# Loads of q, k and v: one DMA over 128 partitions in place of two over 64 each

## The chip, the cores and the metric

One core of a Trainium2 chip runs the kernel. The metric is the device time of the program in microseconds (us). A core has TensorE (PE, with its weight loads shown apart as PEld), VectorE (DVE), ScalarE (ACT), GpSimd (POOL), and SyncE (SP), which here only issues DMAs.

## What is computed

Sigmoid attention over 8 batches of 12 heads, 448 positions and 64 dimensions a head, and then a gated feed-forward block on its result:

```python
def _attn_ref(q, k, v) -> np.ndarray:
    S = q.shape[2]
    scale = 1.0 / np.sqrt(q.shape[-1])
    scores = scale * np.matmul(q, k.transpose(0, 1, 3, 2)) - np.log(S)
    attn = 1.0 / (1.0 + np.exp(-scores))
    return np.matmul(attn, v).astype(np.float32)
...
def _moe_ref(x, w_gate, w_val, w_out) -> np.ndarray:
    g = x @ w_gate
    silu = g * (1.0 / (1.0 + np.exp(-g)))
    val = x @ w_val
    return (silu * val @ w_out).astype(np.float32)
```

x, (3584, 768), is the attention's output with the heads of a position side by side; the weights are 768x1536, 768x1536 and 1536x768.

## The kernel before

**Tiles.** The unit of the attention is a pair set i: four neighbouring heads of one batch (24 sets, three to a batch; QB = 3, NQ = 24). Positions are laid out as 64 partitions times NS = 7: partition p holds positions 7p to 7p + 6 of a head. A tile of q, k or v holds a set as [128, 2, 7, 64] in float32: partition half g and index a tell the head. In the kernel before, head 4r + 2g + a of the batch stands at half g and index a (r is the set's number in its batch); each half is loaded by a DMA of its own (`load`).

**Casts.** q and k are cast to bf16 into a `src` tile (`cast_qk`: DVE and ACT for set 0, DVE for sets 1 and 2, POOL from set 3), v to fp16 (`cast_v`, always POOL; the cast itself is line 199 of `cp`). Weights are cast by POOL as well (lines 250 and 272).

**Attention.** q and k are transposed so that the head's dimensions stand on partitions (64a to 64a + 63 for index a): on PE for sets 0 to 5 (`tr_pe`, line 284), by a DMA transpose issued from SP for the others (`tr_dma`, line 300). For each of the 7 slots s of the keys `burst` makes four score products (line 317) on the four 64x64 quarters of the array: rows by a, columns by g, the result of index a in bank a of the score tile. `sig` (line 331, ACT) takes the sigmoid of both banks at once. `pv` (line 348) multiplies with v, again four products a slot, 28 a set, added up over s in two banks; each of the two banks becomes a tile xT of 128 features (two heads) by 448 positions, cast by DVE or ACT.

**Feed-forward.** `f1` makes, for a batch and one of 12 chunks of 128 hidden features, six products for the gate and six for the value (line 384); ACT, DVE and DVE again (lines 390, 394, 400) make hT of them. `f2` (line 442) multiplies with the output weights, for two batches at a time.

**Order.** The code lists all operations; `list_schedule` orders them by planned durations, slots of the tile rings and a planned DMA time. Each engine then runs its row in order. The DMAs of SP run in this order: q, k and v of sets 0 to 2; then for c = 0 to 3 six loads of weights (384 of the 1536 hidden features) and q, k, v of one more set; from set 6 on a DMA transpose of a set, the loads of the next, and three loads of output weights (sets 7 to 10). Loads land in a ring of 11 staging tiles ("st"), which casts give back; at most 8 DMAs of SP are on their way, a ninth waits for the landing of the first.

Of the kernel before, what the change touches and what calls it, by code (L numbers as in the profile page):

```python
# [9 lines left out]
FP32 = mybir.dt.float32  # L10
FP16 = mybir.dt.float16
# [123 lines left out]
def kernel(  # L135
# [10 lines left out]
    nc = tc.nc  # L146

    B, H, S, D = q.shape
# [4 lines left out]
    NS = 7  # L153
# [8 lines left out]
    psum = ctx.enter_context(tc.tile_pool(name="ps", bufs=1, space=bass.MemoryType.PSUM))  # L162
    one = ctx.enter_context(tc.tile_pool(name="one", bufs=1))
    stg = ctx.enter_context(tc.tile_pool(name="stg", bufs=1))
    sb = ctx.enter_context(tc.tile_pool(name="sb", bufs=1))
    ctx.enter_context(tc.manual_schedule())

    slots = {"A": 2, "TO": 2, "G": 2, "st": 11, "src": 2,
             "v16": 3, "qkT": 3, "pt": 10, "xT": 14, "osb": 2}
# [18 lines left out]
    def op(*a, **kw):  # L188
        o = Op(*a, **kw)
        ops.append(o)  # L190
        return o

    def cp(eng, o, i):
        if eng == "ACT":
            nc.scalar.copy(out=o, in_=i)
        elif eng == "DVE":
            nc.vector.tensor_copy(out=o, in_=i)  # L197
        else:
            nc.gpsimd.tensor_copy(out=o, in_=i)  # L199


    T = {}
    R = {}

    def load(i, nm, src):

        b, r = divmod(i, QB)

        def part(g):
            def fn():  # L210
                if g == 0:
                    T["st_" + nm, i] = stg.tile([128, 2, NS, D], FP32, tag="st", bufs=slots["st"],
                                                name=f"st_{nm}{i}")
                h = 4 * r + 2 * g
                nc.sync.dma_start(  # L215
                    out=T["st_" + nm, i][64 * g:64 * g + 64],
                    in_=src[b][h:h + 2].rearrange("a (p s) d -> p a s d", s=NS))
            return op("SP", 0.5, fn, take=["st"] if g == 0 else [], desc=(128, NS * D * 4))
        R["st_" + nm, i] = [part(0), part(1)]

    def cast_qk(i, nm, eng, parts=None):

# [10 lines left out]
            for e, s0, s1 in parts]  # L233

    def cast_v(i, eng):
        def fn():
            T["v16", i] = sb.tile([128, 2, NS, D], FP16, tag="v16", bufs=slots["v16"], name=f"v16_{i}")
            cp(eng, T["v16", i], T["st_v", i])
        R["v16", i] = op(eng, 0.98, fn, deps=R["st_v", i], take=["v16"], give=R["st_v", i][0].take)

    def load_w(w, dst, c, j2, nm):
        def fl():
# [64 lines left out]
    def burst(ds):  # L307


        def fpe():  # L310
            for i, s in ds:
                sc = psum.tile([128, 2, 512], FP32, tag="A", bufs=2, name="ps_sc")
                qT, kT = T["qkT", i][:, 0], T["qkT", i][:, 1]
                for g in range(2):
                    for a in range(2):
                        r = slice(64 * a, 64 * a + 64)
                        nc.tensor.matmul(  # L317
                            out=sc[64 * g:64 * g + 64, a, 0:S].rearrange("k (s p) -> k s p", s=NS),
                            lhsT=kT[r, s, 64 * g:64 * g + 64], rhs=qT[r, :, 64 * g:64 * g + 64],
                            start=True, stop=True)  # L320
                T["sc", i, s] = sc
        give = [x for i, s in ds if s == NS - 1 for x in R["qkT", i][0].got("qkT")]
        a = op("PE", 0.19 * len(ds), fpe, deps=[x for i in {i for i, _ in ds} for x in R["qkT", i]],
               mode=("Q", "Q"), take=["A"] * len(ds), give=give)
        for n, d in enumerate(ds):
            sig(d, a, a.take[n])

    def sig(key, a, slot):
        def fn():
            pt = sb.tile([128, 2, S], FP16, tag="pt", bufs=slots["pt"], name="pt")  # L330
            nc.scalar.activation(out=pt, in_=T[("sc",) + key][:, :, 0:S], func=SIGM, bias=sb_t,  # L331
                                 scale=qkscale)
            T[("pt",) + key] = pt
        R[("pt",) + key] = op("ACT", 0.95, fn, deps=[a], take=["pt"], give=[slot])

    def pv(i):

        b, r = divmod(i, QB)

        def slots_of(s0, s1):  # L340
            def fn():
                if s0 == 0:
                    for g in range(2):
                        T["pv", i, g] = psum.tile([128, S], FP32, tag="TO", bufs=2, name="ps_pv")
                for s in range(s0, s1):
                    for g in range(2):
                        for a in range(2):
                            nc.tensor.matmul(  # L348
                                out=T["pv", i, g][64 * a:64 * a + 64, :],
                                lhsT=T["v16", i][64 * g:64 * g + 64, a, s, :],  # L350
                                rhs=T["pt", i, s][64 * g:64 * g + 64, a, :],
                                start=(s == 0), stop=(s == NS - 1))
            return fn

        def fx(g):
            def fn():
                t = sb.tile([128, S], FP16, tag="xT", bufs=slots["xT"], name=f"xT_{b}_{2 * r + g}")
                cp(eng[g], t, T["pv", i, g])
                T["xT", b, 2 * r + g] = t
            return fn  # L360
        eng = ("DVE", "ACT" if r == QB - 1 else "DVE")
        pts = [R["pt", i, s] for s in range(NS)]
        cuts = [0, 5, NS] if i < QB else [0, NS]
        vc = R["v16", i]
        for s0, s1 in zip(cuts, cuts[1:]):
            a = op("PE", 0.19 * (s1 - s0), slots_of(s0, s1), deps=pts[s0:s1] + [vc, R.get(("pv", i))],
                   mode=("Q", "Q"), take=["TO", "TO"] if s0 == 0 else [],
                   give=[x for o in pts[s0:s1] for x in o.take] + (vc.take if s1 == NS else []))
            if s0 == 0:
                banks = a.take  # L370
            R["pv", i] = a
        for g in range(2):
            R["xT", b, 2 * r + g] = op(eng[g], 0.62, fx(g), deps=[a], take=["xT"], give=[banks[g]])
# [115 lines left out]
    def loads(i):  # L489
        for nm, src in (("q", q), ("k", k), ("v", v)):  # L490
            load(i, nm, src)

    def casts(i):
        for nm in "qk":
            cast_qk(i, nm, "DVE" if i < CDVE else "POOL")
        cast_v(i, "POOL")
# [5 lines left out]
    cast_qk(0, "k", None, [("DVE", 0, 4), ("ACT", 4, NS)])  # L502
    tr_pe(0, 1)
    cast_v(0, "POOL")

    for what in ORDER:
# [78 lines left out]
    while fpos < B * NF:  # L585
        b, f = divmod(fpos, NF)
# [41 lines left out]
```

## Time and profile before

| | us |
|---|---|
| median of 3 runs (lowest, highest) | 460.97 (460.84, 461.14) |
| the profiled execution | 460.97 |
| its span in the profile | 459.2 |
| PE busy in the span | 427.3 |
| ACT, DVE, POOL busy | 225.1, 168.9, 109.6 |

The span is the stretch from the first to the last instruction of the profiled execution. The table by stage has, after a stage and its length, the busy time of PE, PEld, DVE, ACT and POOL with their instructions. A busy engine counts instructions only, not waits for semaphores. The granted clock is the share of TensorE's full speed (2.4 GHz) that was granted, 0.5 being 1.2 GHz; the record of it begins at about 21 us, and before that the table by stage shows 1.00. The DMA share is the mean busy share of the core's 16 DMA engines; transfers overlap, so it can pass 1. "Idle before" in square brackets is the time for which an engine stood still ahead of an instruction, with what released it.

### The profile page before, as it was taken

How to read it: one execution, taken by the hardware profiler on the slowest of the kernel's cores; microseconds unless marked ns; L12 is line 12 of the kernel's file. 1: busy time of each engine (PE TensorE's matmuls, PEld its weight loads, DVE VectorE, ACT ScalarE, POOL GpSimd, SP SyncE). 2: the span in 40 equal slices, each digit the busy share in tenths (PEclk: the TensorE clock that was granted, in tenths of full speed). 3: DMA queues.
4: the chain of work that ended last, by engine and by line, in shares of the span. 5: the costliest groups of instructions: out<-in, count | busy, mean ns of one | idle time of the engine just before them, and what ended most of it. 6: DMA issues, size and time to landing. Idle time of an engine off the chain costs nothing.

```text
span 459.2 us, 7942 instructions
## 1 busy us (share of the span) xinstructions
PE 427.3 (93%) x3252; PEld 211.7 (46%) x3252; DVE 168.9 (37%) x278; ACT 225.1 (49%) x305; POOL 109.6 (24%) x145
## 2 busy tenths in 40 slices
PE   2873799989999999999999999999999999999995
PEld 1431344444454554554454554554454545554563
DVE  1512354444433333343434333433334333334210
ACT  3782367865646446455546446445546443112111
POOL 1245464443334233020412133111300000000000
PEclk9998799999999999999999999999999999999999
DMA  8999987999989988518859967528701111110144
GB/s 190 260 286 281 267 260 166 276 249 237 264 184 194 156 186 210 128 68 136 126 132 169 127 130 194 131 67 148 121 1 35 36 36 34 36 47 23 34 104 104
DMA packets 65348, 66.97 MB, mean 146 GB/s; under 512 B 36640, under 2 KB 61472, under 8 KB 65312
## 3 DMA queue, kind: packets, MB, share of 16 engines
q1 hardware_dynamic: 63584, 59.39, 58.5%
q0 software_dynamic: 1728, 7.08, 7.0%
q8 instruction: 25, 0.41, 0.4%
q14 instruction: 11, 0.09, 0.1%
HBM read 47.19 MB, written 11.01 MB: 127 GB/s over the span
## 4 chain that ended last, share of the span: by engine, by line
PE 75%; DMA 19%; SPq 3%; POOL 1%; DVE 1%; ACT 1%; issue 0%; POOLq 0%
PE ps_g L384 20%; PE ps_v L384 20%; PE ps_o L442 19%; DMA st_v<-in_v_dram 7%; PE ps_sc L317 6%; PE ps_pv L348 5%; PE ps_ol L442 5%; DMA st_q<-in_q_dram 5%; DMA st_wv<-in_moe_w_val_dram 3%; DMA st_k<-in_k_dram 3%; SPq L215 2%; DMA qkT<-src 1%; DVE t L394 1%; ACT s L390 1%; POOL v L199 0%
## 5 line engine op out<-in xcount | busy, mean ns | idle before, releaser
L331 ACT ACTIVATE pt<-ps_sc,sbiast 128x896 f16<-128x896 f32 x168 | 159.3, 1005 | 38.7 <-PE ps_sc L317 38.6
L384 PE MATMUL ps_v<-xT,wv 128*128 128x448 f16 x576 | 126.8, 356 | 0.1
L384 PE MATMUL ps_g<-xT,wg 128*128 128x448 f16 x576 | 125.0, 353 | 1.2 <-DVE t L394 1.2
L390 ACT ACTIVATE s<-ps_g 128x448 f16<-128x448 f32 x96 | 52.2, 543 | 123.6 <-PE ps_g L384 123.6
L394 DVE TENSOR_TENSOR t<-ps_g,s 128x448 f16<-128x448 f32 x96 | 60.0, 625 | 126.1 <-ACT s L390 126.1
L442 PE MATMUL ps_o<-wo,hT 128*128 128x384 f16 x528 | 92.5, 326 | 0.0
L442 PEld LDWEIGHTS <-hT 128*128 128x128 f16 x672 | 65.8, 98 | 45.7
L400 DVE SCALAR_TENSOR_TENSOR hT<-ps_v,t 128x448 f16<-128x448 f32 x96 | 60.0, 625 | 61.7 <-PE ps_v L384 60.0
L384 PEld LDWEIGHTS <-wg 128*128 128x128 f16 x576 | 54.7, 98 | 56.9 <-issue 9.8
L384 PEld LDWEIGHTS <-wv 128*128 128x128 f16 x576 | 51.3, 98 | 62.4 <-issue 23.0
L317 PE MATMUL ps_sc<-qkT 64*64 64x448 bf16 x672 | 52.3, 375 | 6.0 <-ACT pt L331 3.4
L463 POOL DMA_DIRECT2D out_dram<-osb x36 | 18.7, 525 | 112.6 <-issue 77.7
L199 POOL CAST src<-st_q 128x896 bf16<-128x896 f32 x21 | 19.6, 934 | 85.2 <-DMA st_q<-in_q_dram 84.2
L348 PE MATMUL ps_pv<-pt,v 64*64 64x448 f16 x672 | 38.6, 360 | 0.6 <-ACT pt L331 0.5
L317 PEld LDWEIGHTS <-qkT 64*64 64x64 bf16 x672 | 14.4, 107 | 38.6 <-issue 33.3
L197 DVE CAST xT<-ps_pv 128x448 f16<-128x448 f32 x40 | 23.4, 619 | 22.5 <-PE ps_pv L348 22.5
L199 POOL CAST v<-st_v 128x896 f16<-128x896 f32 x24 | 22.4, 935 | 38.6 <-DMA st_v<-in_v_dram 23.5
L453 ACT ACTIVATE osb<-ps_o 128x384 f32<-128x384 f32 x22 | 10.8, 490 | 39.8 <-PE ps_o L442 39.8
L348 PEld LDWEIGHTS <-v 64*64 64x64 f16 x672 | 19.8, 109 | 16.0 <-issue 4.8
L284 PE MATMUL ps_tr<-idn,src 128*128 128x128 bf16 x84 | 8.6, 258 | 19.2 <-POOL src L199 10.7
L442 PE MATMUL ps_ol<-wo,hT 128*128 128x384 f16 x144 | 24.7, 326 | 0.0
L455 DVE TENSOR_SCALAR osb<-ps_o 128x384 f32<-128x384 f32 x22 | 12.3, 557 | 31.8 <-PE ps_o L442 31.8
(22 smaller groups left out, 80.6 us busy)
## 6 DMA issues: line engine op xcount, KB each, us to landing
st_q<-in_q_dram SPq DMA_DIRECT2D x48, 224.0 KB, 4.9
st_k<-in_k_dram SPq DMA_DIRECT2D x48, 224.0 KB, 5.1
st_v<-in_v_dram SPq DMA_DIRECT2D x48, 224.0 KB, 5.8
out_dram<-osb POOLq DMA_DIRECT2D x36, 192.0 KB, 3.3
st_wg<-in_moe_w_gate_dram SPq DMA_DIRECT2D x12, 384.0 KB, 7.9
st_wv<-in_moe_w_val_dram SPq DMA_DIRECT2D x12, 384.0 KB, 10.0
st_wo<-in_moe_w_out_dram SPq DMA_DIRECT2D x12, 384.0 KB, 6.7
out_dram<-osb SPq DMA_DIRECT2D x18, 192.0 KB, 2.7
```

The source lines that it names most:

```text
L197: nc.vector.tensor_copy(out=o, in_=i)
L199: nc.gpsimd.tensor_copy(out=o, in_=i)
L317: nc.tensor.matmul(out=sc[64 * g:64 * g + 64, a, 0:S].rearrange("k (s p) -> k s p", s=NS), lhsT=kT[r, s, 64 * g:64 * g + 64], rhs=qT[r, :, ...
L331: nc.scalar.activation(out=pt, in_=T[("sc",) + key][:, :, 0:S], func=SIGM, bias=sb_t, scale=qkscale)
L348: nc.tensor.matmul(out=T["pv", i, g][64 * a:64 * a + 64, :], lhsT=T["v16", i][64 * g:64 * g + 64, a, s, :], rhs=T["pt", i, s][64 * g:64 * ...
L384: nc.tensor.matmul(out=T[nm, b, f], lhsT=w[c][:, j, ff * 128:(ff + 1) * 128], rhs=T["xT", b, j], start=(j == 0), stop=(j == KC - 1))
L390: nc.scalar.activation(out=t, in_=T["g", b, f], func=SIGM)
L394: nc.vector.tensor_tensor(out=t, in0=T["g", b, f], in1=T["s16", b, f], op=MULT)
L400: nc.vector.scalar_tensor_tensor(out=T["hT", m, f][:, o * S:(o + 1) * S], in0=T["v", b, f], scalar=HSC, in1=T["t1", b, f], op0=MULT, op1=MULT)
L442: nc.tensor.matmul(out=o, lhsT=T["hT", m, f][:, t * 128:(t + 1) * 128], rhs=wo16[f][:, cs], start=(f == 0), stop=(f == NF - 1))
L455: nc.vector.tensor_scalar_mul(T["osb", m, t][:, c], o, HREC)
L463: dma.dma_start(out=out[rows, c].rearrange("(p s) d -> s p d", s=NS)[s], in_=T["osb", m, t][64 * n:64 * n + 64, c])
```

## The change

`load` issues one DMA for q, k or v of a set instead of two. The tile's partitions now hold neighbouring heads: head 4r + 2a + g stands at half g and index a, so that each index a is one contiguous piece of 128 x 1792 bytes in DRAM. The planner is told of one DMA of 256 runs instead of two of 128.

Scores: the product of index a and key half g now writes the column half g XOR a (it was g), in bank a as before. So for a = 1 the two halves of the keys' partitions hold the heads in exchanged places.

v: the two halves of index a = 1 are exchanged in the cast to match. `cast_v` does it in three POOL instructions (both halves of a = 0, then each half of a = 1 into the other half), planned at 1.75 instead of 0.98.

Value products: the bank is now given by a and the column half by g, the row half by g XOR a; it was bank and row half by g, column half by a.

```diff
@@ -206,17 +206,12 @@
 
         b, r = divmod(i, QB)
 
-        def part(g):
-            def fn():
-                if g == 0:
-                    T["st_" + nm, i] = stg.tile([128, 2, NS, D], FP32, tag="st", bufs=slots["st"],
-                                                name=f"st_{nm}{i}")
-                h = 4 * r + 2 * g
-                nc.sync.dma_start(
-                    out=T["st_" + nm, i][64 * g:64 * g + 64],
-                    in_=src[b][h:h + 2].rearrange("a (p s) d -> p a s d", s=NS))
-            return op("SP", 0.5, fn, take=["st"] if g == 0 else [], desc=(128, NS * D * 4))
-        R["st_" + nm, i] = [part(0), part(1)]
+        def fn():
+            T["st_" + nm, i] = stg.tile([128, 2, NS, D], FP32, tag="st", bufs=slots["st"], name=f"st_{nm}{i}")
+            nc.sync.dma_start(
+                out=T["st_" + nm, i].rearrange("q a s d -> q a (s d)"),
+                in_=src[b][4 * r:4 * r + 4].rearrange("(a g) (p s) d -> (g p) a (s d)", a=2, s=NS))
+        R["st_" + nm, i] = [op("SP", 0.5, fn, take=["st"], desc=(256, NS * D * 4))]
 
     def cast_qk(i, nm, eng, parts=None):
 
@@ -233,10 +228,13 @@
             for e, s0, s1 in parts]
 
     def cast_v(i, eng):
+
         def fn():
-            T["v16", i] = sb.tile([128, 2, NS, D], FP16, tag="v16", bufs=slots["v16"], name=f"v16_{i}")
-            cp(eng, T["v16", i], T["st_v", i])
-        R["v16", i] = op(eng, 0.98, fn, deps=R["st_v", i], take=["v16"], give=R["st_v", i][0].take)
+            t = T["v16", i] = sb.tile([128, 2, NS, D], FP16, tag="v16", bufs=slots["v16"], name=f"v16_{i}")
+            cp(eng, t[:, 0], T["st_v", i][:, 0])
+            for g in range(2):
+                cp(eng, t[64 - 64 * g:128 - 64 * g, 1], T["st_v", i][64 * g:64 * g + 64, 1])
+        R["v16", i] = op(eng, 1.75, fn, deps=R["st_v", i], take=["v16"], give=R["st_v", i][0].take)
 
     def load_w(w, dst, c, j2, nm):
         def fl():
@@ -315,7 +313,7 @@
                     for a in range(2):
                         r = slice(64 * a, 64 * a + 64)
                         nc.tensor.matmul(
-                            out=sc[64 * g:64 * g + 64, a, 0:S].rearrange("k (s p) -> k s p", s=NS),
+                            out=sc[64 * (g ^ a):64 * (g ^ a) + 64, a, 0:S].rearrange("k (s p) -> k s p", s=NS),
                             lhsT=kT[r, s, 64 * g:64 * g + 64], rhs=qT[r, :, 64 * g:64 * g + 64],
                             start=True, stop=True)
                 T["sc", i, s] = sc
@@ -340,16 +338,15 @@
         def slots_of(s0, s1):
             def fn():
                 if s0 == 0:
-                    for g in range(2):
-                        T["pv", i, g] = psum.tile([128, S], FP32, tag="TO", bufs=2, name="ps_pv")
+                    for a in range(2):
+                        T["pv", i, a] = psum.tile([128, S], FP32, tag="TO", bufs=2, name="ps_pv")
                 for s in range(s0, s1):
                     for g in range(2):
                         for a in range(2):
+                            r = slice(64 * (g ^ a), 64 * (g ^ a) + 64)
                             nc.tensor.matmul(
-                                out=T["pv", i, g][64 * a:64 * a + 64, :],
-                                lhsT=T["v16", i][64 * g:64 * g + 64, a, s, :],
-                                rhs=T["pt", i, s][64 * g:64 * g + 64, a, :],
-                                start=(s == 0), stop=(s == NS - 1))
+                                out=T["pv", i, a][64 * g:64 * g + 64, :], lhsT=T["v16", i][r, a, s, :],
+                                rhs=T["pt", i, s][r, a, :], start=(s == 0), stop=(s == NS - 1))
             return fn
 
         def fx(g):
```

The planned order on PE, ACT and DVE is the same before and after, instruction by instruction. On two engines rows differ.

SP at the start of the program: q, k and v of set 0, q and k of set 1 (names: st_ and the tensor with the number of its set), before

```order
L215 DMA st_q0_99<-in_q_dram 64x2x448 x2
L215 DMA st_k0_103<-in_k_dram 64x2x448 x2
L215 DMA st_v0_106<-in_v_dram 64x2x448 x2
L215 DMA st_q1_109<-in_q_dram 64x2x448 x2
L215 DMA st_k1_114<-in_k_dram 64x2x448 x2
```

SP at the same place, after

```order
L211 DMA st_q0_99<-in_q_dram 128x2x448
L211 DMA st_k0_102<-in_k_dram 128x2x448
L211 DMA st_v0_104<-in_v_dram 128x2x448
L211 DMA st_q1_106<-in_q_dram 128x2x448
L211 DMA st_k1_108<-in_k_dram 128x2x448
```

Nothing moved; each load is one instruction where there were two, and the rest of SP's row follows in the same order.

POOL from q of set 3 to q of set 4 (src: the cast q and k; v16: the cast v; wg and wv: gate and value weights of c = 1), before

```order
L199 CAST src1_73<-st_q3_236 128x2x7x64
L199 CAST src1_73<-st_k3_263 128x2x7x64
L199 CAST v16_3_447<-st_v3_283 128x896
L250 CAST wg16_1_80<-st_wg1_0_303 128x768
L250 CAST wg16_1_80<-st_wg1_1_316 128x768
L250 CAST wg16_1_80<-st_wg1_2_333 128x768
L250 CAST wv16_1_84<-st_wv1_0_344 128x768
L250 CAST wv16_1_84<-st_wv1_1_347 128x768
L250 CAST wv16_1_84<-st_wv1_2_359 128x768
L199 CAST src0_72<-st_q4_391 128x2x7x64
```

POOL on the same stretch, after

```order
L199 CAST src1_73<-st_q3_195 128x2x7x64
L199 CAST src1_73<-st_k3_225 128x2x7x64
L199 CAST v16_3_438<-st_v3_235 128x448
L199 CAST v16_3_438<-st_v3_235 64x448 x2
L248 CAST wg16_1_80<-st_wg1_0_266 128x768
L248 CAST wg16_1_80<-st_wg1_1_307 128x768
L248 CAST wg16_1_80<-st_wg1_2_319 128x768
L248 CAST wv16_1_84<-st_wv1_0_338 128x768
L248 CAST wv16_1_84<-st_wv1_1_348 128x768
L248 CAST wv16_1_84<-st_wv1_2_353 128x768
L199 CAST src0_72<-st_q4_385 128x2x7x64
```

The order is the same; the cast of v has become three instructions, and all that follows stands behind them.

## Rows read from the trace of the kernel before

**Rows 1.** The page, part 4: shares of the chain that ended last, by engine.
```profile
PE 75%; DMA 19%; SPq 3%; POOL 1%; DVE 1%; ACT 1%; issue 0%; POOLq 0%
```

**Rows 2.** Table by stage: length, busy us by engine, granted clock, DMA share, GB/s.
```profile
0.00:33.50 33.50, 20.83 (x218) 10.63 (x218) 9.24 (x16) 22.05 (x25) 8.94 (x17) 1.00 1.00 243
...
33.50:48.40 14.90, 3.72 (x33) 1.92 (x34) 3.12 (x5) 3.41 (x5) 8.13 (x10) 0.78 1.07 276
...
103.00:400.00 297.00, 296.78 (x2252) 145.28 (x2250) 115.63 (x190) 153.58 (x211) 65.16 (x88) 1.00 0.63 127
```

**Rows 3.** Time line of PE: start, length, line, operation, idle before, releaser.
```profile
33.09 0.38 PE L348 MATMUL ps_pv<-pt,v 64*64 64x448 f16 x4 [0.51 <-ACT pt L331]
...
35.94 0.56 PE L284 MATMUL ps_tr<-idn,src 128*128 128x128 bf16 x7 [1.21 <-POOL src L199]
...
38.17 1.30 PE L384 MATMUL ps_g<-xT,wg 128*128 128x448 f16 x6 [0.38 <-DVE t L394]
...
48.38 0.93 PE L284 MATMUL ps_tr<-idn,src 128*128 128x128 bf16 x7 [8.91 <-POOL src L199]
...
49.10 2.45 PE L384 MATMUL ps_v<-xT,wv 128*128 128x448 f16 x6
...
52.19 1.31 PE L384 MATMUL ps_g<-xT,wg 128*128 128x448 f16 x6
```

**Rows 4.** Time line of POOL: casts of v (sets 0, 1) and of q, set 4.
```profile
9.51 0.93 POOL L199 CAST v<-st_v 128x896 f16<-128x896 f32 x1 [8.17 <-DMA st_v<-in_v_dram]
...
15.45 0.93 POOL L199 CAST v<-st_v 128x896 f16<-128x896 f32 x1 [5.02 <-DMA st_v<-in_v_dram]
...
47.39 0.93 POOL L199 CAST src<-st_q 128x896 bf16<-128x896 f32 x1 [1.02 <-DMA st_q<-in_q_dram]
```

**Rows 5.** DMA traffic from 4.5 to 17.5 us, by size of packet.
```profile
DMA packets 1897, 3.03 MB, mean 233 GB/s; under 512 B 208, under 2 KB 1897, under 8 KB 1897
```

**Rows 6.** DMA traffic from 21 to 25.5 us, by size of packet.
```profile
DMA packets 1159, 1.68 MB, mean 373 GB/s; under 512 B 77, under 2 KB 1158, under 8 KB 1158
```

**Rows 7.** Groups of POOL's instructions by shape: count, busy us, mean ns, idle before.
```profile
L199 POOL CAST v<-st_v 128x896 f16<-128x896 f32 x24 | 22.4, 935 | 38.6 <-DMA st_v<-in_v_dram 23.5 <-PE ps_pv L348 10.3 <-issue 3.8
...
L250 POOL CAST wg<-st_wg 128x768 f16<-128x768 f32 x12 | 9.9, 827 | 3.9 <-DMA st_wg<-in_moe_w_gate_dram 3.6
```

**Rows 8.** Time line of ACT: the sigmoids of the first three pair sets.
```profile
10.18 2.80 ACT L331 ACTIVATE pt<-ps_sc,sbiast 128x896 f16<-128x896 f32 x3 [2.27 <-PE ps_sc L317]
...
15.61 2.80 ACT L331 ACTIVATE pt<-ps_sc,sbiast 128x896 f16<-128x896 f32 x3 [0.94 <-PE ps_sc L317]
...
19.54 11.14 ACT L331 ACTIVATE pt<-ps_sc,sbiast 128x896 f16<-128x896 f32 x12 [1.13 <-PE ps_sc L317]
...
31.14 1.90 ACT L331 ACTIVATE pt<-ps_sc,sbiast 128x896 f16<-128x896 f32 x2 [0.46 <-PE ps_sc L317]
```

**Rows 9.** Time line of PE: transposes of k, set 1, and the scores behind them.
```profile
14.11 0.93 PE L284 MATMUL ps_tr<-idn,src 128*128 128x128 bf16 x7 [0.49 <-DVE src L197]
...
14.96 0.96 PE L317 MATMUL ps_sc<-qkT 64*64 64x448 bf16 x8
```

**Rows 10.** Time line of PE: the waits between 57 and 103 us.
```profile
63.37 0.56 PE L284 MATMUL ps_tr<-idn,src 128*128 128x128 bf16 x7 [0.56 <-POOL src L199]
...
80.89 0.38 PE L317 MATMUL ps_sc<-qkT 64*64 64x448 bf16 x4 [0.45 <-DMA qkT<-src]
...
93.73 0.57 PE L317 MATMUL ps_sc<-qkT 64*64 64x448 bf16 x8 [1.26 <-DMA qkT<-src]
```

**Rows 11.** Time line of SP's queue: one DMA transpose.
```profile
86.65 2.83 SPq L300 DMA_TRANSPOSE qkT<-src  x1
```

**Rows 12.** Chain that ended last, in order of time: start us, us, what.
```profile
98.86 5.40 DMA qkT<-src
...
109.93 1.45 PE ps_pv L348 x28
...
122.39 1.45 PE ps_pv L348 x28
```

## The prediction

> **What bounds the kernel now.** I read the chain that ended last first, then the table by stage, then the time lines of TensorE (PE), GpSimd (POOL) and ScalarE (ACT) for the first 110 us, and last the DMA traffic of two short stretches. The profiled execution took 460.97 us, which is also the median of the runs; its span is 459.2, so 1.8 us lie around it, and I add them back at the end.
>
> PE's own work is 75% of the chain that ended last, and 19% of it is DMA [rows 1]. The table by stage tells where [rows 2]. From 103 to 400 us PE stands still for 0.2 us in 297, so nothing is to be had there. The idle time is ahead of that: 12.7 us up to 33.5 and 11.2 between 33.5 and 48.4. There the DMA share is 1.00 and more, and POOL, which casts what has landed, is busy for 8.9 of 33.5 and 8.1 of 14.9 us, so what is late is loads. The largest single gap stands in PE's time line [rows 3]: a product of f1 begins at 38.17 and lasts 1.30, then PE waits 8.91 us for POOL's cast of q of pair set 4 (a pair set is one i, four heads) and begins to transpose it at 48.38. POOL began that cast at 47.39, as soon as the load had landed [rows 4]. In the gap the granted clock falls to 1.2 GHz (0.78 is the mean of that stage, [rows 2]): six f1 products take 2.45 us at 49.10, and 1.31 at 52.19, at 2.4 GHz again [rows 3].
>
> **Why the loads are slow.** Between 4.5 and 17.5 us the queue holds nothing but halves of q, k and v: 3.03 MB in 1897 packets, of which 208 are tiny, so 1792 bytes each, at 233 GB/s [rows 5]. Between 21 and 25.5 it holds weights, 128 partitions a load, 1536 bytes a packet, at 373 GB/s [rows 6]. The DMA engines are full in both. The rows differ in two things, the run length and whether a load goes to 64 or 128 partitions; shorter runs were the faster ones, so I put the difference down to the partitions. POOL's casts of v agree: the first two start 5.94 us apart, which is three loads [rows 4], so 2.0 us for a load of 458,752 bytes, or 229 GB/s.
>
> **The change, part by part.**
>
> *One load over 128 partitions.* Same bytes, same 1792-byte runs, half the number of DMAs. Bounds for the rate are 233 GB/s (nothing gained) and 373; I take 360, near the weights' rate, since the new load has their form. A load then takes 1.27 us. Landing of the n-th load was 3.5 + 2.0n us (v of set 0 is the third, at 9.51), so now 3.5 + 1.27n. For q of set 4, 13 loads and 12 weight loads of 393,216 bytes must have moved, 10.68 MB: 29.7 us at 360, so it lands at 33.2, and with its cast of 0.93 [rows 7] it is ready at 34.1. At 300 GB/s it would be ready at 40.0.
>
> The Trainium skill, SBUF — State Buffer, section "Can I just issue two DMAs to hit both halves?", says that two loads to the two halves serialize, and its section on the DMA port swizzle ("Door 1") gives 196 GB/s for 64 partitions and 328 for 128, at 1 MiB. The trace agrees in direction (233 against 373). By the page's 328 the q would be ready at 37.0, and my total below would grow by 1.5 us.
>
> *What PE does until then.* Whether PE can use it at 34.1 depends on the start. There ACT's sigmoids are the pace, 21 of them, some 0.93 us each (2.80 for three, 11.14 for twelve, [rows 8]). The first, at 10.18, follows from k of set 0, the second load, which now lands at 6.0 instead of 7.5: 8.7, and its bank is free at 9.65. Behind it stand in PE's order a score product, the transposes of q of set 1, a score product, the transposes of k of set 1 and the score product of the fifth sigmoid. The transposes waited for their loads (0.49 us for k, [rows 9]); those now land at 8.6 and 9.9, so nothing there waits for data. At the half rate of these instructions (7 transposes take 0.93 us, as at 48.38) a step with transposes is 0.85 (14.11 to 14.96) and one of a score product 0.65 (14.96 to 15.61): 9.65 + 3 x 0.65 + 2 x 0.85 = 13.3 for the fifth sigmoid, which stood at 15.61, 2.3 us gained. The sigmoids behind it follow at ACT's own pace, and the 0.46 us at 31.14, in which PE stood behind weights being cast, goes too. So the last value products of set 2, at 33.09 [rows 3], come at 30.3 and end at 30.7. From there PE needed 6.0 us to the end of the product of 38.17, of which 1.21 was a wait for k of set 3; I keep 4.8, and PE is at the transposes of set 4 at 35.5. That is later than 34.1, so it decides: **gain 48.38 - 35.5 = 12.9 us.** With full clock earlier in the start it would be up to 14.3 (then the q decides); at 300 GB/s it is 8.4.
>
> *The clock.* Without a gap of 8.91 us I see no cause for the fall to 1.2 GHz (at 31 to 39 us, with waits of up to 1.21 us, the products ran at 2.4). From 48.38 to 52.19 PE did 7 transposes, 6 products and 8 score products; the products took 1.1 us more than at 2.4 GHz, and in the same proportion the rest 0.6: **gain 1.7 us.**
>
> *Later waits.* PE waited 0.56 for q of set 5 and 0.45 and 1.26 for DMA transposes [rows 10]. The latter end a chain on SP: transposes, loads, casts, next transposes; its transposes at 86.65 [rows 11] and 98.86 are 12.2 us apart, as long as PE's own period, from one set's value products to the next, 109.93 to 122.39 [rows 12]. With two loads 0.7 us faster each it is some 1.4 us shorter, and it starts earlier: k of set 6 lands after 18.6 MB, at 55.2, casts end at 57, and transposes take 5.4 us [rows 12], so they are there at 62.5; PE wanted them at 80.4 and, moved by 15.2, does so at 65. **Gain 2.3 us**, bounds 0 and 2.3.
>
> *Cast of v in three pieces.* 128x896 takes 935 ns and 128x768 827 [rows 7], so 0.84 ns a column and 0.18 fixed. A piece of 448 columns is then 0.56 us and three are 1.68; no row shows a cast on 64 partitions or one that moves them, so the bounds are 1.68 and, with 0.93 for each moved piece, 2.43. Nor would it be below 0.93, since no column is left out. POOL's work between v of set 2 (the ninth load, landing now at 14.9) and the cast of q of set 4 is two v, twelve weight casts and two others: 15.2 us (16.7 by the upper bound), so it is through at 30.1 (31.6), before q lands at 33.2. Price 0. If that cover went, it would be 0.75 us a set. Behind a longer cast on POOL stand weight casts and output stores; none of them was late after 103 us.
>
> *SP.* Its order stays, with one issue where two stood , and the next load behind each comes earlier. Price 0: the DMA engines are full.
>
> *Score and value products.* Count, shapes and PE's order stay; what changes is which 64x64 quarter of the array a product uses. 28 value products take 1.45 us [rows 12]; 7 rounds of 448 columns at 2.4 GHz are 1.31, so four quarters run at once. In both kernels the four products of a slot use four different quarters. I take 0, with bounds -0.1 and, if only two could run together, +1.3 us a set.
>
> Sum: 12.9 + 1.7 + 2.3 = 16.9; span 459.2 - 16.9 = 442.3; with 1.8 around it 444.1. **I predict 444 us.**
>
> **The rivals.**
>
> *The value products run two at a time (slower).* Before, the upper half of the array's rows wrote one PSUM bank and the lower half the other. Now each bank (one per a) gets products from both row halves in the same slot, in different column halves. No row shows that case. Rows show the other sharing, two column halves in one bank, at no cost. If the two row halves had to take turns, 24 sets would pay 1.3 us each, 31 us in all: 460.97 - 16.9 + 31 = 475. It decides from 0.7 us a set (16.9 / 24). Against it: the four outputs still lie on disjoint halves of partitions per bank. Chance 0.07.
> The Trainium skill, TensorEngine Tiling (Array Packing), section Restrictions and Gotchas, says that different row tiles cannot use the same PSUM bank at once; PSUM — Partial Sum Buffer, section "PSUM bank collisions raise a hardware error", holds that each bank of each partition is a RAM of its own. By the first the time is this rival's, by the second nothing changes.
>
> *The loads don't get faster.* If the 1792-byte runs or the source, not the 64 partitions, set 233 GB/s, q of set 4 lands where it did. One DMA for two frees SP, but the engines were full. POOL's longer cast stays hidden behind the late loads. 461, within 1. Against it: the rate changes with the kind of load in stretches next to each other [rows 5, 6]. Chance 0.04.
>
> *The gap shrinks but another takes its place.* Loads at under 290 GB/s, or a stall in the first 30 us that I did not see: 451 to 459. Chance 0.05.
>
> **How the numbers follow.** My forecast, 440.5 to 451, has 0.84. Its low end is the full clock earlier (-1.4) and value products 0.1 us quicker (-2.4); its high end is 300 GB/s (+4.5) with the later waits kept (+2.3). That range leaves 0.16 out, so it is also the range that I give. About 0.2% is what a measurement of this kernel can tell from no change. Faster by more: 0.84 + 0.05 = 0.89, less 0.01 for a rival that ends at 460 or so: 0.88. Same 0.04. Slower 0.08, the first rival and a share of the second.
>
> **What would show it.** In the changed kernel: 340 to 370 GB/s in the first 17 us and casts of v 3.8 us apart; PE at the transposes of set 4 near 35.5 with no wait over 1.5 us ahead of them; the granted clock at 2.4 GHz through 30 to 60 us; 28 value products in 1.3 to 1.5 us; POOL's pieces near 0.56 us; PE's idle time ahead of the steady part cut by about 14 us. Wrong would be: loads still 2 us apart, value products near 2.6 us, or a new wait of several us between 20 and 60.

## The result, and the profile after

The changed kernel takes 443.18 us, median of four runs (442.80 to 443.43), against 460.90 (460.06 to 461.14) for the kernel before beside it: a ratio of 0.9618, 95% interval 0.9601 to 0.9635. The forecast was 444, with a range of 440.5 to 451. The profiled execution took 443.35 us with a span of 441.6, so 1.75 us lie around the span, as before.

The page of the kernel after: the engines' totals, the granted clock in 40 slices, and the shares of the chain that ended last (the line that answers to [rows 1]). The last line is the clock's row of the kernel before.

```profile
PE 424.7 (96%) x3252; PEld 211.4 (48%) x3252; DVE 168.5 (38%) x278; ACT 224.9 (51%) x305; POOL 127.8 (29%) x193
...
PEclk9999999999999999999999999999999999999999
...
PE 92%; ACT 3%; DMA 2%; DVE 1%; issue 1%; SPq 0%; ACTq 0%
...
PEclk9998799999999999999999999999999999999999
```

PE's share of the chain went from 75% to 92% and that of DMA from 19% to 2%. No slice of the span reads below full clock any more. (For about the first 20 us this row doesn't tell all: it reads full clock there in both kernels, while seven transposes still take 0.93 us at 19.09 and, at 2.4 GHz, 0.56 at 20.27.)

The table by stage of the kernel after, columns as in [rows 2].

```profile
0.00:33.50 33.50, 22.48 (x236) 12.11 (x236) 10.93 (x19) 22.91 (x27) 19.71 (x33) 1.00 0.98 345
33.50:48.40 14.90, 14.53 (x136) 7.09 (x136) 8.02 (x15) 11.05 (x15) 12.58 (x17) 1.00 1.07 375
...
103.00:400.00 297.00, 296.69 (x2212) 146.93 (x2211) 114.66 (x189) 145.58 (x202) 62.22 (x99) 1.00 0.43 105
```

The second column of numbers is PE's busy time: it stands still for 11.0 us in the first stage and 0.4 in the second, where it was 12.7 and 11.2. The DMA engines are as full as before (0.98 and 1.07), and move 345 and 375 GB/s where they moved 243 and 276. Over the first 103 us PE's idle time fell from 26.2 to 11.4 us.

The time line of PE after, around the place where the long gap of [rows 3] stood (start, length, line, operation, and in brackets the idle time before it and what ended that).

```profile
30.80 0.38 PE L347 MATMUL ps_pv<-pt,v 64*64 64x448 f16 x4 [0.51 <-ACT pt L329]
...
34.45 1.29 PE L381 MATMUL ps_g<-xT,wg 128*128 128x448 f16 x6 [0.24 <-DVE t L391]
35.58 0.55 PE L282 MATMUL ps_tr<-idn,src 128*128 128x128 bf16 x7
35.97 1.30 PE L381 MATMUL ps_v<-xT,wv 128*128 128x448 f16 x6
...
37.71 1.31 PE L381 MATMUL ps_g<-xT,wg 128*128 128x448 f16 x6
...
48.16 0.55 PE L282 MATMUL ps_tr<-idn,src 128*128 128x128 bf16 x7
```

The transposes of q of set 4 start at 35.58 instead of 48.38, with no wait ahead of them, and take 0.55 us instead of 0.93, at 2.4 GHz; the products behind them take 1.30 instead of 2.45. The transposes of set 5 (48.16) don't wait either.

GpSimd's time line after, the answer to [rows 4]: the casts of v of sets 0, 1 and 2, each now three pieces, and of q of set 4.

```profile
8.87 2.19 POOL L199 CAST v<-st_v 128x448 f16<-128x448 f32 x3 [7.53 <-DMA st_v<-in_v_dram]
...
12.54 2.25 POOL L199 CAST v<-st_v 128x448 f16<-128x448 f32 x3 [1.48 <-DMA st_v<-in_v_dram]
...
16.16 1.78 POOL L199 CAST v<-st_v 128x448 f16<-128x448 f32 x3 [1.37 <-DMA st_v<-in_v_dram]
...
33.57 0.93 POOL L199 CAST src<-st_q 128x896 bf16<-128x896 f32 x1 [0.48 <-PE ps_v L381]
```

The casts of v are 3.67 and 3.62 us apart, where the first two stood 5.94 apart: 1.22 us for a load instead of 2.0. The q of set 4 is cast by 34.50 instead of 48.32. GpSimd still stands idle for 0.48 us ahead of that cast. The row puts this down to a product of PE, but the load, issued at 24.79, took 8.6 us to land, so it came in at 33.4, and the load is most likely what the cast waited for.

DMA traffic after, from 4.5 to 14 us, in which the queue holds q, k and v alone (it was 4.5 to 17.5 in [rows 5]):

```profile
DMA packets 2021, 3.38 MB, mean 356 GB/s; under 512 B 122, under 2 KB 2021, under 8 KB 2021
```

The time line of ACT after, the answer to [rows 8], the sigmoids of the first three sets:

```profile
8.20 2.80 ACT L329 ACTIVATE pt<-ps_sc,sbiast 128x896 f16<-128x896 f32 x3 [2.26 <-PE ps_sc L315]
...
13.57 2.80 ACT L329 ACTIVATE pt<-ps_sc,sbiast 128x896 f16<-128x896 f32 x3 [0.37 <-PE ps_sc L315]
...
17.51 11.17 ACT L329 ACTIVATE pt<-ps_sc,sbiast 128x896 f16<-128x896 f32 x12 [1.13 <-PE ps_sc L315]
...
28.84 1.90 ACT L329 ACTIVATE pt<-ps_sc,sbiast 128x896 f16<-128x896 f32 x2 [0.17 <-PE ps_sc L315]
```

PE's waits (what it waited for, total, times, longest): the first three of the list after, and two lines of the list before. Neither GpSimd's casts of q and k (10.7 us in three waits before) nor the DMA transposes (1.9 us in three) stand in the list after.

```profile
PE ps_tr L282 <- DVE src L197: 5.8, 3, 4.6
PE ps_sc L315 <- ACT pt L329: 3.2, 6, 0.7
PE ps_g L381 <- DVE t L391: 1.0, 6, 0.2
...
PE ps_tr L284 <- POOL src L199: 10.7, 3, 8.9
...
PE ps_sc L317 <- DMA qkT<-src: 1.9, 3, 1.3
```

The chain that ended last, after: value products, the answer to [rows 12], and the last output products.

```profile
92.32 1.45 PE ps_pv L347 x28
104.78 1.45 PE ps_pv L347 x28
...
433.00 3.91 PE ps_ol L439 x24
```

The value products stood at 109.93 and 122.39, so 17.61 us are gained by here, and the spans differ by 17.6: everything was gained in the first 92 us. From there the two kernels run alike, 12.46 us from one of these two sets to the next in both.

### The profile page after: what moved, and what is told of

Read it like the earlier page. It is cut to its first block, busy times and chain, and to the rows that moved or that the text cites. A ratio compares the mean times of both kernels' runs of the same rounds, so it can differ in the third digit from the quotient of the medians.

```text
span 441.6 us, 7888 instructions
## 1 busy us (share of the span) xinstructions
PE 424.7 (96%) x3252; PEld 211.4 (48%) x3252; DVE 168.5 (38%) x278; ACT 224.9 (51%) x305; POOL 127.8 (29%) x193
## 4 chain that ended last, share of the span: by engine, by line
PE 92%; ACT 3%; DMA 2%; DVE 1%; issue 1%; SPq 0%; ACTq 0%
PE ps_g L381 25%; PE ps_v L381 25%; PE ps_o L439 19%; PE ps_sc L315 9%; PE ps_pv L347 7%; PE ps_ol L439 5%; ACT pt L329 2%; DMA st_q<-in_q_dram 2%; PE ps_tr L282 1%; DVE t L391 1%; ACT s L387 1%; SPq L211 0%; DVE src L197 0%; ACT xT L195 0%; DVE osb L452 0%
## 5 line engine op out<-in xcount | busy, mean ns | idle before, releaser
L381 PE MATMUL ps_v<-xT,wv 128*128 128x448 f16 x576 | 125.5, 354 | 0.0
L199 POOL CAST v<-st_v 64x448 f16<-64x448 f32 (+1 forms) x72 | 41.0, 569 | 32.6 <-PE ps_pv L347 17.6
L315 PEld LDWEIGHTS <-qkT 64*64 64x64 bf16 x672 | 14.2, 107 | 36.0 <-issue 33.4
L450 ACT ACTIVATE osb<-ps_o 128x384 f32<-128x384 f32 x22 | 10.8, 490 | 39.8 <-PE ps_o L439 39.8
L439 PE MATMUL ps_ol<-wo,hT 128*128 128x384 f16 x144 | 24.7, 326 | 0.0
L199 POOL CAST src<-st_k 128x896 bf16<-128x896 f32 x21 | 19.6, 932 | 5.0 <-DMA st_k<-in_k_dram 4.3
```

The source lines that it names most:

```text
L315: nc.tensor.matmul(out=sc[64 * (g ^ a):64 * (g ^ a) + 64, a, 0:S].rearrange("k (s p) -> k s p", s=NS), lhsT=kT[r, s, 64 * g:64 * g + 64], ...
L381: nc.tensor.matmul(out=T[nm, b, f], lhsT=w[c][:, j, ff * 128:(ff + 1) * 128], rhs=T["xT", b, j], start=(j == 0), stop=(j == KC - 1))
L439: nc.tensor.matmul(out=o, lhsT=T["hT", m, f][:, t * 128:(t + 1) * 128], rhs=wo16[f][:, cs], start=(f == 0), stop=(f == NF - 1))
```

## The experiments

Each is the changed kernel with one edit (the last one with two). Four of them (halves, two by index, weights in halves, whole cast) ran beside the kernel before on one chip, where that took 460.60 us in the median of 19 runs (457.19 to 464.25). The other four shared another chip, where it took 459.82 (458.87 to 460.76).

**Every load as two halves of 64 partitions again, all else of the change kept.**

```diff
-        def fn():
-            T["st_" + nm, i] = stg.tile([128, 2, NS, D], FP32, tag="st", ...)
-            nc.sync.dma_start(
-                out=T["st_" + nm, i].rearrange("q a s d -> q a (s d)"),
-                in_=src[b][4 * r:4 * r + 4].rearrange("(a g) (p s) d -> (g p) a (s d)", a=2, s=NS))
+        def part(g):
+            ...
+                nc.sync.dma_start(
+                    out=T["st_" + nm, i][64 * g:64 * g + 64].rearrange("q a s d -> q a (s d)"),
+                    in_=src[b][4 * r:4 * r + 4].rearrange("(a g) (p s) d -> g p a (s d)", a=2, s=NS)[g])
...
+        R["st_" + nm, i] = [part(0), part(1)]
```

> The changed kernel with each load split again into two DMAs over 64 partitions each; the new layout of heads, the cast of v in three pieces and the new quarters of the products stay. Theory (the 64 partitions of a load set its rate): q, k and v move at about 233 GB/s again, casts of v start about 6 us apart in the first 20 us, PE waits 8 to 10 us for q of set 4 near 40 us, total 459 to 462 us. Rival (the gain came from the layout, the products or the order): the total stays at 443 to 446.

Measured: 459.59 us (456.43 to 460.58), ratio 0.9974 (0.9943 to 1.0005): the gain is gone, and what is left of a difference isn't clear of the noise. Its DMA traffic from 4.5 to 17.5 us, the wait of PE in its time line, and its stage from 33.5 to 48.4 us:

```profile
DMA packets 1992, 3.17 MB, mean 244 GB/s; under 512 B 222, under 2 KB 1992, under 8 KB 1992
```

```profile
45.82 0.93 PE L286 MATMUL ps_tr<-idn,src 128*128 128x128 bf16 x7 [8.02 <-POOL src L199]
```

```profile
33.50:48.40 14.90, 5.94 (x41) 2.94 (x39) 3.65 (x6) 2.88 (x4) 9.07 (x12) 0.72 1.08 288
```

The rate, the gap of 8 us and the fall of the clock (0.72 in this stage, transposes at 0.93 us) all return with the halves. The layout of the heads, the cast in three pieces and the order of the value products are those of the changed kernel here. By themselves they are worth at most the 0.6% that the interval leaves, against the 3.8% of the change, so the gain is that of the loads.

**Two loads again, but split by index a, each over all 128 partitions.** Number and size of the DMAs are those of the kernel before, and the runs are the same 1792 bytes.

```diff
+        def part(a):
+            ...
+                nc.sync.dma_start(
+                    out=T["st_" + nm, i][:, a].rearrange("q s d -> q (s d)"),
+                    in_=src[b][h:h + 2].rearrange("g (p s) d -> (g p) (s d)", s=NS))
...
+        R["st_" + nm, i] = [part(0), part(1)]
```

> The changed kernel with each load split by the index a into two DMAs, each over all 128 partitions: as many DMAs of the same size (224 KB) as before the change, with the same limit of 8 on their way, but 128 partitions. Theory (partitions): 350 to 375 GB/s, total 443 to 445 us. Rival (half as many DMAs, or more bytes on their way under the limit of 8, made the loads faster): 233 to 300 GB/s, total 450 to 461.

Measured: 444.16 us (442.66 to 444.31), ratio 0.9645 (0.9586 to 0.9704). Its traffic from 4.5 to 14 us:

```profile
DMA packets 2182, 3.47 MB, mean 365 GB/s; under 512 B 243, under 2 KB 2182, under 8 KB 2182
```

That two loads became one is not what helped, nor that each is twice as large. That a load goes to 128 partitions and not to one half of them is. Whether the count matters or which 64 they are, no run here tells.

**The weights' loads split into halves of 64 partitions; q, k and v as in the changed kernel.**

```diff
-            nc.sync.dma_start(
-                out=T[nm, c, j2],
-                in_=w[j2 * 256:(j2 + 1) * 256, c * CW:(c + 1) * CW].rearrange(
-                    "(j p) f -> p j f", p=128))
+            for n in range(2):
+                nc.sync.dma_start(
+                    out=T[nm, c, j2][64 * n:64 * n + 64],
+                    in_=w[j2 * 256:(j2 + 1) * 256, c * CW:(c + 1) * CW].rearrange(
+                        "(j n p) f -> n p j f", n=2, p=64)[n])
```

> The changed kernel with each load of gate or value weights split into two DMAs over 64 partitions (runs of 1536 bytes as before, 192 KB a DMA); q, k and v as in the change. Theory (partitions, whatever the data and the run length): the weights fall from about 375 to about 233 GB/s, a load of weights takes 1.7 us instead of 1.05, q of set 4 is ready near 40.7 us, PE waits 4 to 6 us there and a little more at sets 5 and 6, total 448 to 452 us. Rival (runs of 1792 bytes, or the layout of q, k and v in DRAM, were the slow part): weights stay above 350 GB/s, total 443 to 444.

Measured: 457.37 us (454.61 to 460.18), ratio 0.9931 (0.9888 to 0.9973). The direction is right, the size is not: nearly the whole gain is lost. Its traffic from 21 to 25.5 us (the weights), PE's two waits, and GpSimd's casts of q, k and v of set 3:

```profile
DMA packets 735, 1.06 MB, mean 235 GB/s; under 512 B 70, under 2 KB 735, under 8 KB 735
```

```profile
45.22 0.93 PE L283 MATMUL ps_tr<-idn,src 128*128 128x128 bf16 x7 [9.69 <-POOL src L199]
...
61.27 0.67 PE L283 MATMUL ps_tr<-idn,src 128*128 128x128 bf16 x7 [2.00 <-POOL src L199]
```

```profile
28.75 0.93 POOL L199 CAST src<-st_q 128x896 bf16<-128x896 f32 x1 [0.18 <-DMA st_q<-in_q_dram]
31.01 0.93 POOL L199 CAST src<-st_k 128x896 bf16<-128x896 f32 x1 [1.33 <-DMA st_k<-in_k_dram]
33.15 1.78 POOL L199 CAST v<-st_v 128x448 f16<-128x448 f32 x3 [1.20 <-DMA st_v<-in_v_dram]
```

The halves make the weights slow, at 235 GB/s, as expected. What was not expected is in the last fence: the q, k and v between them go to 128 partitions, and still land 2.1 to 2.3 us apart, where in the changed kernel the casts of q, k and v of set 4 start 1.2 us apart (33.57, 34.78, 35.96). The half loads in this queue slow the landings of the full loads among them too. So the whole mixture goes at the slow rate (262 GB/s in the first 33.5 us, 247 in the next stage), and pricing each load by its own kind, as I did here, makes such a mixture too cheap.

**The weights' loads split by rows of the weight instead, two loads of 192 KB over 128 partitions**, the control for the run before.

```diff
+            for n in range(2):
+                nc.sync.dma_start(
+                    out=T[nm, c, j2][:, n],
+                    in_=w[j2 * 256 + n * 128:j2 * 256 + (n + 1) * 128, c * CW:(c + 1) * CW])
```

> The changed kernel with each load of gate or value weights split into two DMAs of 192 KB, each over all 128 partitions (by the two row blocks of the load): the count and size of the split into halves of e3, without the 64 partitions. Theory (64 partitions make loads slow): 350 to 375 GB/s up to 33 us, total 443 to 445 us, so that nearly all of the 14 us that e3 lost is due to the partitions. Rival (more DMAs of 192 KB under the limit of 8 on their way leave the DMA engines short of work): total 448 to 457 us, DMA share dips as in e3.

Measured: 443.79 us (442.35 to 444.50), ratio 0.9646 (0.9620 to 0.9673). Its first two stages, columns as in [rows 2]:

```profile
0.00:33.50 33.50, 22.82 (x246) 12.34 (x247) 12.09 (x21) 23.65 (x28) 19.33 (x33) 1.00 0.97 332
33.50:48.40 14.90, 14.85 (x134) 7.27 (x133) 8.14 (x14) 10.73 (x14) 10.95 (x15) 1.00 1.00 337
```

As many weight loads of the same size as in the run before, and the gain is whole: its loss there is due to the 64 partitions. The time is the expected one; the rate, 332 GB/s in the first stage, is below the 350 to 375 that I expected.

**The cast of v in one instruction.**

```diff
-            cp(eng, t[:, 0], T["st_v", i][:, 0])
-            for g in range(2):
-                cp(eng, t[64 - 64 * g:128 - 64 * g, 1], T["st_v", i][64 * g:64 * g + 64, 1])
+            cp(eng, t, T["st_v", i])
```

> The changed kernel with v cast in one instruction of 128x896, without the exchange of halves; it leaves the exchange out, so the value products pair the wrong heads. Theory (POOL's longer cast is covered): total within 0.5 us of the changed kernel, 442.7 to 443.7 us, with POOL busy 18 us less. Rival (the pieces delay weights or transposes): 1 to 3 us faster than the changed kernel.

Measured: 442.90 us (442.57 to 443.27), ratio 0.9625 (0.9568 to 0.9682), beside 0.9618 for the changed kernel. First its page's totals, then the groups of GpSimd's pieces in the changed kernel (busy us, mean ns):

```profile
PE 422.6 (96%) x3252; PEld 210.3 (48%) x3252; DVE 168.6 (38%) x278; ACT 224.7 (51%) x305; POOL 109.9 (25%) x145
```

```profile
L199 POOL CAST v<-st_v 64x448 f16<-64x448 f32 x48 | 27.6, 574 | 2.9
L199 POOL CAST v<-st_v 128x448 f16<-128x448 f32 x24 | 13.4, 560 | 29.7 <-PE ps_pv L347 17.6 <-DMA st_v<-in_v_dram 12.1
```

The three pieces cost GpSimd 41.0 us for 24 sets where the whole cast costs 22.4 (24 times 0.935), and 17.9 us less work on that engine moved the end by nothing that can be measured. The exchange in the cast has no price that shows, as long as GpSimd has the room.

**PSUM banks of the value products given out by row half**, as in the kernel before: each bank is then written from one half of the array's rows only.

```diff
-                                out=T["pv", i, a][64 * g:64 * g + 64, :], lhsT=T["v16", i][r, a, s, :],
+                                out=T["pv", i, g ^ a][64 * g:64 * g + 64, :], lhsT=T["v16", i][r, a, s, :],
```

> The changed kernel with the bank of a value product given by the row half again (g XOR a), so that no bank gets products from both row halves; it leaves the order of the heads wrong in two of four quarters, so the feed-forward part gets its features in another order. Theory (sharing a bank between row halves costs nothing): 28 value products take 1.45 to 1.52 us as in the changed kernel, total within 0.5 us of 443.2. Rival (the sharing has a price): value products quicker and the total 1 us or more below the changed kernel.

Measured: 442.44 us (442.12 to 443.28), ratio 0.9624 (0.9602 to 0.9645). The median is 0.74 us below the changed kernel's, where I expected 0.5 at most, but on another chip; the ratio to the kernel before beside it is the same (0.9618). Value products and the last output products in its chain, and two rows of PE's time line:

```profile
103.58 1.45 PE ps_pv L347 x28
122.71 1.32 PE ps_pv L347 x28
...
431.79 3.91 PE ps_ol L439 x24
```

```profile
14.56 1.14 PE L347 MATMUL ps_pv<-pt,v 64*64 64x448 f16 x20
...
34.36 0.56 PE L282 MATMUL ps_tr<-idn,src 128*128 128x128 bf16 x7 [0.40 <-POOL src L199]
```

Value products take as long as in the changed kernel (1.45 at 104.78, 1.32 at 123.92). From the transposes of set 4 to the last output products, a stretch with the value products of 21 sets, it is 397.43 us here and 397.42 in the changed kernel (35.58 to 433.00). What sets the two profiles 1.2 us apart lies ahead of it: here TensorE ran at 2.4 GHz from about 14 us on, so that the twenty value products of 14.56 take 1.14 us, and 2.13 in the changed kernel (14.96). The banks aren't the reason, since in the run with the whole cast, which has the changed kernel's banks, they take 1.14 too (14.72). So the two row halves writing one bank, in different halves of its partitions, cost nothing that shows, where the rival priced it at 31 us.

**Warm up: 32 products of the identity with itself, before the first data.**

```diff
+    ps_w = psum.tile([128, 512], FP32, tag="G", bufs=2, name="ps_w")
+    for n in range(32):
+        nc.tensor.matmul(out=ps_w[:, 0:128], lhsT=idn, rhs=idn, start=True, stop=True)
```

> The changed kernel with 32 products of the identity matrix with itself on PE ahead of the first transposes, their result unused. Theory (of the start, the part that is left is paced by PE's instructions at 1.2 GHz until about 20 us): transposes and score products run at 2.4 GHz from about 6 us on, sets 0 and 1 get through 1 to 2.5 us sooner, total 440.5 to 442.3 us. Rival (landings and ACT's sigmoids alone pace the start): total 442.7 to 443.7.

Measured: 443.36 us (442.78 to 443.82), ratio 0.9640 (0.9621 to 0.9661): no gain. Two groups of transposes from PE's time line:

```profile
6.41 0.56 PE L282 MATMUL ps_tr<-idn,src 128*128 128x128 bf16 x7 [0.81 <-DVE src L197]
...
10.42 0.93 PE L282 MATMUL ps_tr<-idn,src 128*128 128x128 bf16 x7 [0.64 <-DVE src L197]
```

The clock did rise (0.56 us for seven transposes at 6.41), but after waits of 0.6 to 0.9 us, for data and for ACT's banks, they took 0.93 at 10.42. The table of two stretches (the third number from the end is the granted clock) shows the fall from 2.4 to 1.2 GHz:

```profile
5.00:9.00 4.00, 1.74 (x22) 1.07 (x21) 1.58 (x3) 1.38 (x2) 0.42 (x1) 0.97 0.95 311
9.00:12.00 3.00, 2.17 (x18) 1.14 (x18) 1.70 (x3) 2.02 (x4) 1.65 (x3) 0.50 1.05 397
```

The fifth sigmoid came at 13.29 instead of 13.57, and PE kept this lead of 0.3 us up to the last gate products ahead of set 4 (34.14 instead of 34.45). There it was lost. GpSimd's cast of q of set 4:

```profile
34.53 0.93 POOL L199 CAST src<-st_q 128x896 bf16<-128x896 f32 x1 [1.57 <-DMA st_q<-in_q_dram]
```

In this profile the q landed 1 us later than in the changed kernel (cast at 33.57), and the transposes of set 4 could start at 35.52 only, instead of 35.58. Why it landed late is open.

**The same warm-up, and q and k of set 1 loaded ahead of v of set 0**, so that PE would not wait for q of set 1.

```diff
-    loads(0)
+    for i in range(2):
+        load(i, "q", q)
+        load(i, "k", k)
+    load(0, "v", v)
```

> As e7, and q and k of set 1 are loaded ahead of v of set 0. Theory: besides the clock, PE's wait for q of set 1 (0.86 us at 10.7 us in the changed kernel) goes, 0.3 to 1 us more than e7, total 439.8 to 442 us. Rival: v of set 0 lands too late for its products instead, total equal to e7 or above.

Measured: 443.36 us (443.12 to 443.63), ratio 0.9639 (0.9616 to 0.9662). ACT's first sigmoids and PE's wait for set 4:

```profile
9.68 6.39 ACT L329 ACTIVATE pt<-ps_sc,sbiast 128x896 f16<-128x896 f32 x7 [4.00 <-PE ps_sc L315]
```

```profile
34.78 0.56 PE L282 MATMUL ps_tr<-idn,src 128*128 128x128 bf16 x7 [1.12 <-POOL src L199]
```

The planner answered the new order of loads by putting the transposes of q of set 1 ahead of the scores of set 0. The first sigmoid is 1.5 us later (8.20 to 9.68), then seven run without a gap, and PE, now early, waits 1.12 us for the cast of q of set 4. Behind it the planned order of PE differs from the changed kernel's. So this run doesn't tell what the order of loads alone is worth; it shows only that it brought nothing as built.

## Why the prediction was right, step by step

**Bound.** That the loads set the end of the first 48 us, and nothing but PE the rest, holds: 17.61 us are gained by the value products at 92.32, where the spans differ by 17.6, and one edit to the loads alone (the halves) takes it back. When the transposes of set 4 begin decides the rest: from there to the last output products it is 397.42 to 397.45 us in the profiles of the changed kernel and of the runs by index, by rows, with the whole cast, with the banks by row half and with the warm-up.

**The rate.** I put the difference between 233 and 373 GB/s down to 64 against 128 partitions, from two neighbouring stretches that differed in run length as well, and took 360; it measured 356 in the first stretch and 375 in the later stage. The runs by index and by halves settle the reason: two DMAs of the old size over 128 partitions go at 365, and over 64 at 244. The Trainium skill, SBUF — State Buffer, section "Can I just issue two DMAs to hit both halves?", says that loads to the two halves serialize; the runs here agree so far that two halves in one queue stayed at 233 to 244 GB/s. The 328 GB/s that the page's section on the DMA port swizzle ("Door 1") gives for 128 partitions at 1 MiB is below what this queue of 448 KB loads moved (356), so the measurement decides.

**When q is ready.** Predicted 34.1, measured 34.50 at the end of its cast (33.57 and 0.93). That this is so close is in part luck: the first loads came late (below), and from the cast of v of set 0 at 8.87 to that of q of set 4 the queue brought 10 loads of q, k and v and 12 of weights, 9.31 MB in 24.7 us or 377 GB/s, where I had 360. The margin of 1.4 us before PE wants it came out at 1.1, so in this profile the start decides, as I said, and not the q. In three others it is the q: with two loads by index, the whole cast and the banks by row half TensorE's clock was up sooner, and PE waited 0.34, 0.98 and 0.40 us for the cast of q and began set 4 at 34.56, 35.13 and 34.36. The prediction had this case as its "full clock earlier", with a gain of up to 14.3 us; the largest is 48.38 - 34.36 = 14.0.

**PE's way there.** Transposes of set 4 at 35.5, measured 35.58: a gain of 12.80 us where 12.9 stood. Two errors lie in it and cancel. The last value products of set 2 came at 30.80, not 30.3, and the way from there took 4.78 us, not 5.2. In the start the fifth sigmoid stood at 13.57 against 13.3, and of the gap of 0.46 us that I had go entirely, 0.17 stayed (28.84). The 13.57 hides two more: the first sigmoid stood at 8.20, not 8.7, and PE then waited for a load, which comes next.

**The first loads.** The rule 3.5 + 1.27n was wrong for the first of them: v of set 0 was cast at 8.87, not 7.3, and PE waited 0.86 us for q of set 1 at 10.70, where I had no wait for data. In the runs with weights in halves and with the whole cast the same v came as late (8.82, 8.76). With the weights split by rows, where the loads of q, k and v are the same, it was cast at 7.44, so the form of these loads isn't the reason. Why is open. It cost nothing that shows in the end: that run took 443.79 us, a ratio of 0.9646 against 0.9618.

**The clock.** From the transposes of set 4 to the gate products behind them (52.19 before, 37.71 now) it took 3.81 us and takes 2.13: 1.68 for the clock, where 1.7 stood.

**Later waits.** Predicted 2.3 as the sum of 0.56, 0.45 and 1.26; all three are gone. From those gate products to the value products of 92.32 (109.93 before) it took 57.74 us and takes 54.61, so 3.13 were gained. The step was short by 0.8: there was a third wait for DMA transposes before, of 0.22 at 104.30, and the four waits cost more than their idle time, together 2.49. The four stretches that hold them took 1.87, 2.37, 2.56 and 2.15 us before and take 1.15, 1.75, 1.23 and 1.73. Two of the waits split a group of score products; the rest is most likely that instructions which overlap without a wait no longer do so with one.

The sum is 12.80 + 1.68 + 3.13 = 17.61 against 16.9, and the two spans differ by 17.6. The 0.7 us between forecast and measurement is that last term. (The low end of the range, 440.5, adds up to 440.3 from its own terms, 444.1 - 1.4 - 2.4.)

**What was put at nothing.** The pieces of the cast: 0.57 and 0.56 us, predicted 0.56, hidden (the run with the whole cast). One exception: the first two casts took 2.19 and 2.25 us, and the third 1.78. VectorE was casting during the first two (10.02 and 13.75) and not during the third; whether that is the reason was not tried. SP: its DMA transposes at 56.10, 65.21 and 74.35 are 9.1 us apart, less than the 10.8 that I worked out, and PE doesn't wait for them.

**The rivals.** Value products two at a time: refuted, 28 take 1.45 us in the chain of either kernel, and giving the banks out the old way left the stretch with 21 sets of them at 397.4 us. The rule of the Trainium skill on row tiles and PSUM banks (TensorEngine Tiling (Array Packing), section Restrictions and Gotchas) does not hold here where the two row halves write different partitions; the one of PSUM — Partial Sum Buffer, section "PSUM bank collisions raise a hardware error", that each bank in each partition is a RAM of its own, agrees with it. Loads that don't get faster: refuted by 356 against 233. Another gap in the place of the first: none, the waits of PE behind 31 us are all below 0.7.

## What to carry to other kernels

When DMA engines are full and loads still come late, compare the rates of two stretches next to each other whose loads have different forms; here a load over 64 partitions moved 233 to 244 GB/s and the same bytes over 128 moved 356 to 375, however many DMAs they were cut into. One kind of half load was enough to slow the mixed queue here, so look at all of them. It is worth paying for the full width elsewhere: here it cost 41.0 us of casts on GpSimd instead of 22.4, all of it hidden, and bought 17.6 us.

## What the runs showed of the hardware that was not expected

Full loads that are queued among half loads land late as well: 2.1 to 2.3 us apart in the run with the weights in halves, about 1.2 without them. The same stands in the kernel before, the other way round: there the half loads are q, k and v, and the last three weights ahead of q of set 4 were cast at 41.77, 43.63 and 45.54, 1.9 us apart, though weights alone went at 373 GB/s [rows 6]. What happens inside the queue was not tried.

A cast on 64 partitions that moves them to the other half takes GpSimd 574 ns for 448 columns, and one on 128 partitions in place takes 560: here half the partitions save nothing, and the move costs nearly nothing.

The clock of TensorE did not stay up on a few products ahead of time: after 32 of them seven transposes took 0.56 us, and four us later, behind waits of 0.6 to 0.9 us, 0.93 again, with the granted clock falling from 0.97 to 0.50.

When it first rises differs between profiles of nearly the same program. In the changed kernel seven transposes at 19.09 us still take 0.93; in the run with the banks by row half twenty value products take 1.14 us, full speed, at 14.56. This moves the start of set 4, and with it the end, by up to 1.2 us. Why was not tried.
